# The first step of a recurrence before a feed-forward block: idle products out, two levels in one PSUM tile, three loads moved

## The chip, the cores and the metric

The kernel runs on one core of a Trainium2 chip. The metric is the device time of one execution in microseconds (us). Engines are named as in the profile: PE is TensorE (PEld its weight loads), DVE is VectorE, ACT is ScalarE, POOL is GpSimd, SP is SyncE, which here only issues DMAs.

## The reference, cut to what matters

A recurrence with decay for 4 batches, 8 heads, 768 tokens and head dimension 48, followed by a gated feed-forward block on its output.

```python
for t in range(S):
    cur = einsum('bhd,bhe->bhde', u * k[t], v[t])
    y[t] = einsum('bhd,bhde->bhe', r[t], state + cur)
    state = w[t][..., None] * state + einsum('bhd,bhe->bhde', k[t], v[t])
x = y laid out as (B * S, H * D) = (3072, 384)
h = x @ w_in                      # 384 -> 2048
g = h * erf(softplus(h))
out = g @ w_out                   # 2048 -> 384
```

## The kernel before, in words

The work is cut into 12 steps. A step holds 128 tokens (`C`) of two batches, 16 head matrices in all, in eight pairs of heads (`JP`), two heads side by side on the partitions. R, K and the decay w of a step lie with the head dimension on the partitions and the tokens along the free axis. The pairs are split into two halves, one for each batch (`j` 0 and 1).

The products of tokens with earlier tokens of the same chunk of 64 are made in six levels (`LOG = 6`). At level n the tokens fall into blocks of 2^n; the right half of a block is multiplied with its left half. For this `level_products` (matmuls at L552) writes 64 x 32 products for each pair, head and chunk to a PSUM tile `pp`; `scale` (L321 for step 0, L328 later) then multiplies R of the right halves and K of the left halves in place by running products of w, so that the next level's products carry the right decay. `take_level` brings the level's products into the SBUF tile `own`: up to level five with a masked DVE copy (L562), at level six with two ACT copies (L569). Level one uses other operands, `rk1`, in which R or K are multiplied by u, and is taken with a DVE multiplication by a mask (L774). The running products of w (`tot_sb`) are made on POOL by `totals` (L350), each behind a one-element copy `wait_for` (L769) which waits for a scale on DVE.

PSUM tiles come from `products`, which hands out two tiles in turn (`pp0`, `pp1`).

Step 0 has a function of its own, `attend_first`. It goes through the levels, then turns K by eight PE transposes (L816) into PSUM, copies the result to `kT` (half on ACT, half on DVE, L821), multiplies `own` with v into `y` (`from_own`, L584), makes the state products K x v (L659), applies the state of the first chunk to the second (`through_state`, L610) and leaves the last part of that (`hop`, three matmuls at L625) and the state of the second chunk to step 1. `fence` copies a few elements of `y` to `seen` (L593) and so waits until `from_own` is done.

Between these operations step 0 holds matmuls whose result nobody reads. `stay_warm` (L862) multiplies an identity; it stands six times at the start and twice after each half of level one. `keep_busy` (L871) multiplies zeros into the next PSUM tile; it stands after each of the levels two to five and before the transposes.

The weights w_in and w_out come as 64-bit floats and are converted on the chip: `convert` has stages that load a pair of blocks ("l"), scale its high words on ACT ("b"), its low words on ACT ("r"), shift on DVE ("h") and add on POOL ("o"). A load can be put behind an element of some tile: a one-element copy on POOL or ACT (L240, L238) into the buffer makes the DMA wait for it. A pair is 0.79 MB in two DMAs; three pairs fit into the buffers.

From step 1 on, `attend` runs the same levels, and pieces of `hidden` (w_in products, L1027) of the step before stand between them. Every engine's order of work is the order of the program text; nothing is reordered. All loads named here are issued by SP from one queue, in order.

Of the kernel before, what the change touches and what calls it, by code (L numbers as in the profile page):

```python
# [17 lines left out]
P = 128  # L18
# [43 lines left out]
def kernel(  # L62
# [68 lines left out]
    def products(shape, n=None):  # L131


        if n is not None:
            return ps_p.tile(shape, FP32, name=f"pp{n}")
        n = turns["next"]
        turns["next"] = 1 - n
        return ps_p.tile(shape, FP32, name=f"pp{n}")
# [10 lines left out]
    def load_w(s):  # L149
        ws[s] = ins.tile([P, JP, C], FP32, name="w")  # L150
        nc.sync.dma_start(out=ws[s][:], in_=rkw[s][:, 2])
# [34 lines left out]
    def load_v(s):  # L186

        vt = loaded[s][1]
        nc.sync.dma_start(out=vt[:], in_=v[s])
# [122 lines left out]
    def scale(s, level, batch=None):  # L312
# [16 lines left out]
            halves, halves, view(tots[level - 1], 0, [[1, n], [2, nb], [0, half]])  # L329
        )  # L330

    def plan_totals(s):


        tots, pairs, tot = [], [], ws[s][:].rearrange("p n t -> p (n t)")
        tot_sb = att.tile([P, JP * (C - NC)], FP32, name="tot_sb")
        used = 0
        for level in range(1, LOG + 1):
            tots.append(tot)
            nb = JP * C >> level  # L340
            new = tot_sb[:, used : used + nb]
            pairs.append((new, tot.rearrange("p (n two) -> p n two", two=2)))
            tot = new
            used += nb
        ready[s] = *ready[s], tots, tot

        def go_on(*levels, part=slice(None)):
            for level in levels:
                new, pair = pairs[level - 1]
                nc.gpsimd.tensor_mul(new[:, part], pair[:, part, 0], pair[:, part, 1])  # L350

        return go_on
# [183 lines left out]
    def first_pair(x, n):  # L536

        return turns["first"][:, n // NP, x, n % NP]
# [19 lines left out]
    def take_level(own, pp, level):  # L558
        half = 1 << (level - 1)
        got = pp[:].rearrange("p e n t -> p (e n) t")  # L560
        if level <= MASKED:
            nc.vector.copy_predicated(  # L562
                rights(own[:], half),
                rights(mask_sb[:, level - 1 : level, :].to_broadcast([P, NH, HC]), half),
                got[..., : HC // 2].rearrange("p n (b h) -> p n b h", h=half),
            )
        else:
            for s0 in range(0, C, HC):
                nc.scalar.copy(own[s0 : s0 + half, :, half:], got[s0 : s0 + half, :, :half])  # L569
# [28 lines left out]
    def through_state(s, xT):  # L598

        c, in_t, _, _, S, _, _ = parts_of(s)  # L600
        for h, state in enumerate((S, middle)):
            if not (c or h):
                continue
            t = slice(h * HC, (h + 1) * HC)
            for j, q in ((0, 2), (1, 2), (1, 0), (0, 0)) if not s else np.ndindex(NJ, NP // 2):
                q = q if not s else 2 * q
                for e in range(NE):
                    for p in (q + e, q + 1 - e):
                        n = j * NP + p
                        nc.tensor.matmul(  # L610
                            y[at(e, p), e, p // 2, j, t],
                            lhsT=state[rows(e), n, :],
                            rhs=(in_t[:, 0, n] if s else first_pair(0, n))[rows(e), t],
                            start=False, stop=True, skip_group_check=True,
                        )

        y3 = att.tile([P, UNIT], FP32, name="y3", bufs=1)
        nc.scalar.copy(y3[:].rearrange("p (j t) -> p j t", j=NJ), y[:, 1, 1])
        parts = y[:, 0, 0], y[:, 0, 1], y[:, 1, 0]
        by_kk = [xT[:, kk, :].rearrange("p (j t) -> p j t", j=NJ) for kk in range(KT)]  # L620
        if not s:

            def hop():
                for kk in range(KT):
                    nc.tensor.matmul(  # L625
                        parts[kk], lhsT=apart[:, kk],
                        rhs=y3[:].rearrange("p (j t) -> p j t", j=NJ),
                        start=False, stop=True, skip_group_check=True,
                    )
                for kk in range(KT):  # L630
                    nc.scalar.copy(by_kk[kk], parts[kk])
                stages["l"](3, xT[:, KT - 1, 0:1], True)
                stages["l"](4)
                load_w(2)

            turns["hop"] = hop
            return
        for kk in range(KT):
            nc.scalar.copy(by_kk[kk], parts[kk])
        by_scalar = {(kk, 1) for kk in range(KT) if s <= DIRECT}  # L640
        for kk in range(KT):
            n = D // KT
            for e in range(NE):
                queue = nc.scalar if (kk, e) in by_scalar else nc.sync
                queue.dma_start(
                    out=xT[e * EP + D : (e + 1) * EP, kk, :],
                    in_=y3[e * EP + kk * n : e * EP + (kk + 1) * n, :],
                )
# [97 lines left out]
    def attend_first(xT):  # L746
# [10 lines left out]
        pp = products([P, NE, JP, HC])  # L757
        for half in halves:
            level_products(pp, by_pair(made), 1, half)
            stay_warm(2)  # L760
        nc.scalar.copy(first[:], mask_sb[:, 0, :])
        totals(1, part=slice(0, batch))
        for j in range(NJ):
# [3 lines left out]
        def wait_for(t):  # L767

            nc.gpsimd.tensor_copy(out=block_sb[:, 0:1], in_=t5[:, 1, 0, NP - 1, t : t + 1])  # L769
# [9 lines left out]
        for level in range(2, LOG):  # L779
            pp = turns.pop("pp", None) or products([P, NE, JP, HC])  # L780
            for j, half in enumerate(halves):
                level_products(pp, first_pair, level, half)
                scale(0, level, batch=j)
            turns["pp"] = products([P, NE, JP, HC])
            keep_busy(turns["pp"], (DM,))
            take_level(own, pp, level)
            wait_for(1 << level - 1)
            if level == 2:
                totals(2, part=slice(batch // 2, batch))
            else:  # L790
                totals(*behind[level])
            if level == 2:
                stages["b"](0, 0)
                stages["b"](0, 1)
                stages["r"](0)
                for _ in prepare(1):
                    pass
                nc.sync.dma_start(out=vt[:], in_=v[0])
                stages["l"](1, own[:, 0, 2:3])
                nc.sync.dma_start(out=ws[1][:], in_=rkw[1][:, 2])  # L800
        totals = plan_totals(1)
        pp = turns.pop("pp")
        for j, half in enumerate(halves):
            level_products(pp, first_pair, LOG, half)
            scale(0, LOG, batch=j)
        take_level(own, pp, LOG)

        kT = att.tile([P, NH, D], FP32, name="kT", bufs=1)
        kT_by_e = kT[:].rearrange("p (e n) d -> p e n d", e=NE)
        turned = [products([P, NE, JP, HC])]  # L810
        keep_busy(turned[0], (DM,))
        for j, half in enumerate(halves):
            if j:
                turned.append(products([P, NE, JP, HC]))
            for i, n in enumerate(half):
                nc.tensor.transpose(  # L816
                    turned[j][:, 0, 2 * i : 2 * i + 2], first_pair(1, n), ident[:]
                )
        from_own(0, own, 1)
        for half, ps, copy in zip(halves, turned, (nc.scalar.copy, nc.vector.tensor_copy)):  # L820
            copy(  # L821
                kT_by_e[:, :, half.start : half.stop],
                ps[:, 0].rearrange("p (n e) d -> p e n d", e=NE)[..., :D],
            )
        stages["b"](1, 0)
        stages["b"](1, 1)
        fence()
        stages["l"](2, seen[:, 0:1])
        load_v(1)
        stages["h"](0)  # L830
        stages["h"](0)
        ps = [[products([P, NE, JP, HC], 1 - e)[:, e] for e in range(NE)]]
# [4 lines left out]
        stages["r"](1)  # L837
        stages["h"](1)
        stages["h"](1)
        wait_for(HC - 1)  # L840
        stages["o"](0)
        nc.gpsimd.tensor_mul(faded[1][:], middle[:], ends[:, :, 1:2].to_broadcast([P, JP, D]))
        totals(1)
# [14 lines left out]
    def stay_warm(times):  # L858

        for _ in range(times):  # L860
            ps = ps_m.tile([P, NC, P], FP32, name="m")
            nc.tensor.matmul(  # L862
                ps[:], lhsT=ident[:], rhs=ident[:, None, :].to_broadcast([P, NC, P]),
                start=True, stop=True,
            )

    def keep_busy(pp, columns=(DM, DM // 2)):

        zeros = states[1][0][:].rearrange("p n d -> p (n d)")
        for n in columns:  # L870
            nc.tensor.matmul(  # L871
                pp[:].rearrange("p e n t -> p (e n t)")[:, :n], lhsT=ident[:],
                rhs=zeros[:, :n], start=True, stop=True, skip_group_check=True,
            )
# [722 lines left out]
```

## Time and profile before

| | us |
|---|---|
| median of 3 runs | 585.62 |
| lowest, highest | 584.13, 586.57 |
| the profiled execution | 586.88 |
| its span | 585.1 |

| busy in the span | share |
|---|---|
| PE | 99% |
| DVE | 78% |
| ACT | 61% |
| POOL | 47% |

The profiled execution is one run; its own time is 1.8 us longer than the span from the first to the last instruction. The lines of its page give busy times. A line of the timeline gives the start and the length of a group of like instructions in us from the start of the span, then engine, line, operation, output and inputs, shape and count; where the engine stood idle before it, a bracket gives for how long and what ended the wait ("issue": nothing that the profile shows). A matmul of fp32 counts as two passes in the counts of the trace, a transpose as one.

### The profile page before, as it was taken

What the parts mean: (1) busy time and instruction counts of PE and PEld (TensorE: products, weight loads), DVE (VectorE), ACT (ScalarE), POOL (GpSimd) and SP (SyncE); (2) the same over time, 40 slices, a digit from 0 to 9 for tenths busy, and PEclk for the clock granted to TensorE, in tenths of its full rate; (3) what the DMA queues carried; (4) which work ended last, traced back from release to release, by engine and by line L of the source; (5) the groups of instructions that cost most, each with busy time, mean ns of one, the idle gap of its engine ahead of it and who ended that gap; (6) DMA issues with size and microseconds to landing.
All of it is one profiled execution on the core that took longest, in us unless ns stands there. A gap on an engine that the chain in (4) does not pass through costs nothing.

```text
span 585.1 us, 16663 instructions
## 1 busy us (share of the span) xinstructions
PE 576.4 (99%) x7240; PEld 495.1 (85%) x7240; DVE 454.7 (78%) x558; ACT 355.6 (61%) x478; POOL 274.1 (47%) x313
## 2 busy tenths in 40 slices
PE   8899999999999999999999999999999999999997
PEld 6588887688668758998898898898898899988997
DVE  6776886999996899799799799799799637256630
ACT  3658877644544598756766666665765771387700
POOL 4557391702398469659459459449549200000000
PEclk9999999999999999999999999999999999999999
DMA  8587571440433414334334334334331301000000
GB/s 269 177 273 281 201 235 44 183 154 10 145 95 116 117 55 156 63 116 165 74 111 169 74 108 172 75 108 136 74 108 55 74 8 36 2 0 2 28 27 29
DMA packets 54082, 63.25 MB, mean 108 GB/s; under 512 B 35160, under 2 KB 40568, under 8 KB 52984
## 3 DMA queue, kind: packets, MB, share of 16 engines
q1 hardware_dynamic: 53624, 61.98, 33.4%
q8 instruction: 57, 0.93, 0.6%
q10 hardware_dynamic: 384, 0.20, 0.1%
q14 instruction: 17, 0.14, 0.1%
HBM read 52.39 MB, written 8.69 MB: 104 GB/s over the span
## 4 chain that ended last, share of the span: by engine, by line
PE 95%; DVE 3%; issue 1%; ACT 0%; POOL 0%; DVEq 0%; POOLq 0%
PE m L1027 36%; PE m L1142 28%; PE m L1059 8%; PE pp L552 6%; PE pp L1230 4%; PE y L1230 2%; PE y L584 2%; PE pp L659 2%; PE y L610 2%; PE m L862 1%; PE pp L871 1%; PE pp L938 1%; DVE in L328 1%; DVE words L467 1%; PE pp L1142 0%
## 5 line engine op out<-in xcount | busy, mean ns | idle before, releaser
L1027 PE MATMUL m<-xT,w_in_sb 128*128 128x256 f32 x960 | 215.3, 382 | 0.1
L1027 PEld LDWEIGHTS m<-xT,w_in_sb 128*128 128x128 f32 x960 | 179.9, 190 | 26.2 <-issue 1.0
L328 DVE TENSOR_TENSOR in<-in,tot_sb 128x1024 f32<-128x1024 f32 (+1 forms) x55 | 75.3, 1369 | 16.5 <-PE pp L552 13.2
L463 POOL TENSOR_TENSOR rk<-words 128x528 f32<-128x528 f32 (+3 forms) x28 | 42.5, 1517 | 91.2 <-DVE sums L453 80.7
L1036 ACT COPY h<-m 128x512 f32<-128x512 f32 x80 | 46.4, 579 | 57.6 <-PE m L1027 57.5
L467 POOL TENSOR_TENSOR words<-words,rest 128x528 f32<-128x528 f32 (+10 forms) x77 | 78.1, 1015 | 6.0
L1059 PE MATMUL m<-w_out_sb,h 128*128 128x384 f32 x192 | 64.3, 491 | 0.0
L1059 PEld LDWEIGHTS m<-w_out_sb,h 128*128 128x128 f32 x192 | 35.7, 190 | 23.5
L1142 PE MATMUL m<-mixed,h 128*128 128x192 f32 x256 | 45.6, 331 | 0.0
L1142 PE MATMUL m<-w_out_sb,h 128*128 128x192 f32 x256 | 44.8, 329 | 0.0
L552 PEld LDWEIGHTS pp<-in 48*64 48x64 f32 (+1 forms) x2368 | 33.4, 126 | 12.0 <-issue 6.2
L1142 PEld LDWEIGHTS m<-mixed,h 128*128 128x128 f32 x256 | 41.4, 190 | 0.9
L1142 PEld LDWEIGHTS m<-w_out_sb,h 128*128 128x128 f32 x256 | 41.6, 190 | 0.3
L1142 PE MATMUL m<-w_out_sb,room 128*128 128x192 f32 x240 | 41.5, 326 | 0.0
L983 ACT ACT_TABLE_LOAD x30 | 38.5, 1283 | 2.7 <-issue 2.2
L987 ACT ACT_TABLE_LOAD x30 | 38.5, 1283 | 1.5 <-DVE room L1125 1.1
L1142 PEld LDWEIGHTS m<-w_out_sb,room 128*128 128x128 f32 x240 | 39.4, 190 | 0.0
L402 POOL TENSOR_TENSOR tot_sb<-tot_sb 128x256 f32<-128x256 f32 (+4 forms) x50 | 36.2, 724 | 3.8
L552 PE MATMUL pp<-in 48*64 48x32 f32 (+1 forms) x2368 | 37.3, 212 | 0.6 <-DVE in L328 0.5
L463 POOL TENSOR_TENSOR words<-words 128x336 f32<-128x336 f32 (+6 forms) x49 | 35.3, 720 | 3.8
L453 DVE TENSOR_REDUCE sums<-rk 128x14 f32<-128x672 f32 (+9 forms) x54 | 34.7, 701 | 0.0
L453 DVE TENSOR_REDUCE sums<-words 128x6 f32<-128x288 f32 (+8 forms) x66 | 26.9, 464 | 3.9 <-POOL words L463 3.6
(198 smaller groups left out, 951.5 us busy)
## 6 DMA issues: line engine op xcount, KB each, us to landing
in<-in_rkw SPq DMA_DIRECT2D x8, 1024.0 KB, 5.1
words<-in_moe_w_in SPq DMA_DIRECT2D x16, 384.0 KB, 5.4
words<-in_moe_w_out SPq DMA_DIRECT2D x16, 384.0 KB, 4.7
words<-in_rk_rows SPq DMA_DIRECT2D x8, 768.0 KB, 5.6
w<-in_rkw SPq DMA_DIRECT2D x11, 512.0 KB
v<-in_v SPq DMA_DIRECT2D x12, 384.0 KB, 5.6
out<-o SPq DMA_DIRECT2D x23, 192.0 KB, 2.4
in<-in_rkw SPq DMA_DIRECT2D x7, 512.0 KB, 5.7
```

The costliest lines, as they stand in the source:

```text
L328: nc.vector.tensor_mul(halves, halves, view(tots[level - 1], 0, [[1, n], [2, nb], [0, half]]))
L402: nc.gpsimd.tensor_mul(new, pair[:, :, 0], pair[:, :, 1])
L453: nc.vector.tensor_reduce(out=view(sums[:], n, [[near * (NEAR + 1), NEAR // near], [NEAR + 1, near - n]]), in_=terms[n], axis=mybir.AxisLi ...
L463: engine.tensor_mul(terms[n], r[:, :, n:], k[:, :, : near - n])
L467: engine.tensor_mul(k[:, :, :m], k[:, :, :m], w[:, :, n : n + m])
L552: nc.tensor.matmul(to, lhsT=rk(1, n)[rows(e), s0 : s0 + m], rhs=right, start=True, stop=True,)
L983: nc.scalar.activation(sp_room, chunks[0], AF.Softplus)
L987: nc.scalar.activation(at, sp_room, AF.Erf)
L1027: nc.tensor.matmul(ps[:, ff, :], lhsT=w_in_sb[:, g * FG + f + ff, kk * P : (kk + 1) * P], rhs=xT[:, kk, :], start=kk == 0, stop=kk == KT - 1,)
L1036: nc.scalar.copy(h[:, f : f + FT, :], ps[:])
L1059: nc.tensor.matmul(ps[j][:], lhsT=gs[g][:, f, j * C : (j + 1) * C], rhs=w_out_sb[:, g * FG + f, :], start=g + f == 0, stop=g == NG - 1 and ...
L1142: nc.tensor.matmul(to, lhsT=a[:, f], rhs=b[:, f], start=start and f == 0, stop=f == FG - 1, skip_group_check=True,)
```

## The change

- The two `stay_warm` products after each half of level one are removed, as are the `keep_busy` products before level six and before the transposes.
- Level six writes its products to the unused half of level five's PSUM tile (`pp[:, :, :, 32:]`) instead of a tile of its own.
- The last scale is split: K first, for each half (`scale_last(K=True)`), and R later, only for the second chunk's right half, which is all that is read afterwards.
- Level six is brought into `own` before level five, level five's copy stands behind K's scales, and R's scale behind that copy.
- All eight transposes go to one PSUM tile, a bank for each half.
- The load of w of step 1 is issued before the second pair of w_in blocks instead of after it. The third pair of blocks waits for the first element of `kT` instead of `seen`. v of step 1 is loaded in `hop`, after w of step 2, instead of after the third pair.
- The `wait_for` before the first weight addition looks at token 127 instead of 63.

```diff
+    def scale_last(K, batch=0):
+        half, nb = 1 << (LOG - 1), 2 * NP
+        of, tot = turns["first"][:, batch], ready[0][1][LOG - 1]
+        if K:
+            keys = view(of, NP * C, [[2 * half, nb], [1, half]])
+            nc.vector.tensor_mul(
+                keys, keys, view(tot, 2 * batch * nb + 1, [[2, nb], [0, half]])
+            )
+            return
+        queries = view(of, 3 * half, [[2 * NP * C, NJ], [C, NP], [1, half]])
+        nc.vector.tensor_mul(
+            queries, queries, view(tot, 2, [[2 * nb, NJ], [4, NP], [0, half]])
+        )
...
                 stages["l"](3, xT[:, KT - 1, 0:1], True)
                 stages["l"](4)
                 load_w(2)
+                load_v(1)
...
             level_products(pp, by_pair(made), 1, half)
-            stay_warm(2)
...
-            turns["pp"] = products([P, NE, JP, HC])
-            keep_busy(turns["pp"], (DM,))
-            take_level(own, pp, level)
+            if level < LOG - 1:
+                turns["pp"] = products([P, NE, JP, HC])
+                keep_busy(turns["pp"], (DM,))
+                take_level(own, pp, level)
...
                 nc.sync.dma_start(out=vt[:], in_=v[0])
+                nc.sync.dma_start(out=ws[1][:], in_=rkw[1][:, 2])
                 stages["l"](1, own[:, 0, 2:3])
-                nc.sync.dma_start(out=ws[1][:], in_=rkw[1][:, 2])
         totals = plan_totals(1)
-        pp = turns.pop("pp")
+        last = pp[:, :, :, HC // 2 :]
         for j, half in enumerate(halves):
-            level_products(pp, first_pair, LOG, half)
-            scale(0, LOG, batch=j)
-        take_level(own, pp, LOG)
+            level_products(last, first_pair, LOG, half)
+            scale_last(K=True, batch=j)
+        take_level(own, last, LOG)
+        take_level(own, pp, LOG - 1)
+        scale_last(K=False)
...
-        turned = [products([P, NE, JP, HC])]
-        keep_busy(turned[0], (DM,))
+        turned = products([P, NE, JP, HC])
         for j, half in enumerate(halves):
-            if j:
-                turned.append(products([P, NE, JP, HC]))
             for i, n in enumerate(half):
                 nc.tensor.transpose(
-                    turned[j][:, 0, 2 * i : 2 * i + 2], first_pair(1, n), ident[:]
+                    turned[:, j, 2 * i : 2 * i + 2], first_pair(1, n), ident[:]
                 )
         from_own(0, own, 1)
...
+        stages["l"](2, kT[:, 0, 0:1])
         stages["b"](1, 0)
         stages["b"](1, 1)
         fence()
-        stages["l"](2, seen[:, 0:1])
-        load_v(1)
...
-        wait_for(HC - 1)
+        wait_for(C - 1)
```

## The prediction

> **What bounds the kernel now.** I read the page's busy shares first, then the busy times of three stretches, then the timelines of PE and DVE in the first 30 us.
>
> ```profile
> PE 576.4 (99%) x7240; PEld 495.1 (85%) x7240; DVE 454.7 (78%) x558; ACT 355.6 (61%) x478; POOL 274.1 (47%) x313
> ...
> 7.10:20.60 13.50, 12.82 (x405) 9.14 (x405) 12.11 (x17) 6.95 (x17) 5.43 (x14) 1.00 0.82 261
> 20.60:29.90 9.30, 6.68 (x208) 5.30 (x205) 4.58 (x10) 5.53 (x13) 6.76 (x6) 1.00 0.44 150
> 29.90:60.90 31.00, 30.99 (x664) 25.71 (x666) 21.00 (x22) 21.66 (x35) 19.24 (x25) 1.00 0.75 261
> ```
>
> The stretches list PE, PEld, DVE, ACT, POOL, the granted clock, the DMA share and GB/s. From 29.9 us PE is full (30.99 of 31.00), and over the whole span it is 99% busy. So what step 0 saves before the first piece of `hidden` (L1027 at 29.89) arrives at the end one for one, unless step 1 can't feed PE. Inside step 0 PE's fullness is false: part of it is idle products (L862, L871), and DVE is busy 12.11 of 13.50.
>
> ```profile
> 9.76 1.23 DVE L774 TENSOR_TENSOR own<-pp,first 128x1024 f32<-128x1024 f32 x1 [0.77 <-PE pp L552]
> 11.41 1.30 DVE L321 TENSOR_TENSOR in<-in,tot_sb 128x512 f32<-128x512 f32 x2 [0.42 <-PE pp L552]
> ...
> 17.61 1.34 DVE L321 TENSOR_TENSOR in<-in,tot_sb 128x512 f32<-128x512 f32 x2
> 18.87 0.70 DVE L562 COPY_PREDICATED own<-mask_sb,pp 128x512 f32<-128x512 int32 x1
> 19.48 1.27 DVE L321 TENSOR_TENSOR in<-in,tot_sb 128x512 f32<-128x512 f32 x2
> 21.57 0.56 DVE L821 COPY kT<-pp 128x384 f32<-128x384 f32 x1 [0.82 <-PE pp L816]
> ```
>
> Two waits for PE stand before level two; after them DVE runs without a gap to 20.75, 1.93 us a level (13.77, 15.71, 17.61, 19.48). Now PE after the levels:
>
> ```profile
> 18.73 0.76 PE L552 MATMUL pp<-in 48*32 48x32 f32 x64
> 19.72 0.88 PE L871 MATMUL pp<-s,ident 128*128 128x384 f32 x2 [0.24 <-DVE own L562]
> 20.44 1.09 PE L816 MATMUL pp<-ident,in 128*128 128x128 f32 x8
> 21.46 0.66 PE L584 MATMUL y<-own,v 64*48 64x64 f32 x32
> 22.27 0.65 PE L659 MATMUL pp<-v,kT 64*48 64x48 f32 x20
> 23.81 0.43 PE L659 MATMUL pp<-v,kT 64*48 64x48 f32 x11 [0.88 <-issue]
> ...
> 29.40 0.56 PE L552 MATMUL pp<-rk 48*64 48x64 f32 x18 [1.26 <-issue]
> ```
>
> PE stops twice in the middle of a group, for nothing that the profile names. Between the two stops the timeline counts 128 matmuls (12 and 32 to through 24.7, 32 of L610, 32 of L552, 6 of L625, 14 of L552), each with its weight load: 256 instructions.
>
> **What the Trainium skill says.** "Runtime: NRT & Kernel Launch", Instruction fetch mechanics: instructions come in blocks of 16 KiB (256 of them), fetched while the block before is executed, at a cost "mostly hidden". The trace agrees on the block and not on the hiding: the page's queue q8 moves 57 packets of 0.93 MB, and narrow windows of the DMA view find one of them starting at 15.7, 21.6, 27.0 and 32.5; PE resumes 2.2 and 2.4 us after the second and third. "DMA: Bandwidth & Descriptors", Queues, rings and completion order: a DMA engine takes turns between queues, a packet at a time. The trace fits: with loads in flight the third and fourth packets come 3.2 and 3.1 us after PE entered the block before (23.81, 29.40). "SBUF — State Buffer", Who interferes with whom: a DVE operation with two SBUF inputs and a POOL read exclude each other. Here the first scale of level one took 1.12 us beside POOL, its twin 0.68. "TensorE: Matmul & The Clock Gate", Part 1: PE falls to half clock after about an idle window of 3.4 us. The clock here is 1.00 throughout, and no stretch that the change opens is over 1 us but by a stall.
>
> **The change, part by part** (clock of the profiled execution).
>
> *Idle products at level one.* Four matmuls of two passes, 1.06 us a pair in the chain, 2.12 us of PE. Level one then ends at 8.6 instead of 9.6; level two needs DVE's scale of level one, which ends at 9.00 as before (it waits for w, landed 7.2). `own` (L774) starts at 9.0, not 9.76, and the level-two scale follows it: its first half by 10.1 instead of 11.41. DVE's chain moves **1.3 us** earlier, not 2.1. POOL's totals of level two are ready at 10.2 and later ones hang on DVE, so they move along.
>
> *Levels five and six in one tile.* The idle product between them goes (0.84), and its wait for the level-four copy. Level five's scale is done at 17.6; level six runs 17.0 to 18.2 (19.5 before). K's two scales are 128x256 each, 0.42 by the row of that shape (L372) against 0.67, and end at 18.7; the transposes end at 19.4 (21.5 before). But the order of writes to `own` turns round: level six's ACT copies (2 x 0.58) come first, and DVE's level-five copy, which overlaps them, must wait. ACT is free at 18.3, as before, since it multiplies step 1's R and K from 14.6 on, when they land. So: ACT copies to 19.4, level-five copy 19.5 to 20.2, R's scale (256 elements, 0.42) to 20.5, kT's DVE copy to 21.0; `from_own` 20.3 to 20.95, `seen` 21.05. The state products start at 21.1 instead of 22.27: still **1.15** early. Level six's own gain is eaten by its ACT copies; behind the waiting DVE copy stand R's scale, the kT copy and `seen`.
>
> *Transposes in one tile*, and R scaled only in the second half: one bank wait less, 0 us; the idle product before them (0.84) was cover.
>
> *Three loads.* w of step 1 is issued at 10.6 instead of 17.13, ahead of the second weight block; that block at about 13.9; the third behind the first kT copy, at about 20 instead of 22.64, through POOL's 0.18 us copy, which waits there with nothing due behind it. v of step 1 goes from 23.50 to behind `load_w(2)`. None is waited for on the path: w is used at 25.7, v at 52.6. They shift DMA traffic against the instruction blocks. After the change 10 to 12 passes fewer stand before the block boundaries, so these fall at level six's fifth matmul, at the end of the state products, and in step 1's level one.
>
> *If every block came in time*: state products to 22.2; ACT `b(1)` to 22.7, middle to 23.2; rest of `through_state` to 23.8; ACT's r(1) and y3 to 24.5; the three hop products to 26.1; xT to 27.05; first piece at 27.1 instead of 29.89, **2.8 us**.
>
> *But the boundary in level six.* Its block is requested when the sequencer enters level four, at about 13.2 to 13.8, and w now flows until about 16 (1.96 MB from 10.5 at the 0.36 MB/us of that stretch). By the traced delays it starts between 1.2 us (lightly loaded: 14.5 to 15.7) and 3.2 us later and is usable 2.2 us after that: 16.6 to 19.2, against 17.05 needed. I cost it at a stall of 1.3 (bounds 0 and 2.5). The following blocks find a quieter DMA queue (the second weight block ends by 18.5) and are then just in time: the 0.88 and most of the 1.26 stay saved. 2.8 less 1.3, less 0.2 for what remains, is **1.3 us**.
>
> *Step 1.* DVE and PE run there without slack: level five's products (45.32) follow the scale that ends 45.26, which follows a shift waiting for ACT and a weight load landed 42.3. v adds 0.39 MB (1.1 us) behind the hop; DMA has idle room at 36 to 38. Cost 0 to 0.7; taken as within the rounding.
>
> Sum: 586.88 less 1.3 is 585.6 for the profiled execution, which stands 1.26 above the median of 585.62; from the median, **584.3 us**.
>
> **The rivals.**
> (B) No stall at level six, none later: 2.8 us, **582.8**. For it: the sequencer may run ahead of the waits (the 15.7 packet served 17.89 just in time). Against: w in flight where before the queue had emptied at 14.9.
> (C) The other side: the stall at level six lasts 2.5 us, since level six is on the path of K's scales, transposes and state products. These then start at 23.4, 1.2 later than before, and if step 1's block stalls too (the old 1.26), the first piece starts at 30.4: +0.5, **586.1**. It decides from a block usable later than about 19, with the next stall uncovered.
> (D) The gain is real and step 1's weight stream gives it back: v and w2 delay the block for level five by about 1 us, leaving 0.3: **585.3**.
> That the idle products kept the clock up is no case of its own, since no idle window is long enough; it stands behind the chance of slower.
>
> **How the numbers follow.** 0.5% of this kernel, 2.9 us, is about what a measurement can tell from no change. Chances: likeliest 0.52 (own range 583.2 to 585.4), B 0.27, C 0.13, D 0.08. Runs shown spread from 584.1 to 586.6, so each case is blurred by about 0.8. The range takes B with that blur below and C above: 582.2 to 586.5. Faster by over 0.5% (below 582.7) is half of B and a little of A: 0.16; slower, beyond 588.5, only C together with a lost clock: 0.04; within, 0.80.
>
> **What would show it.** Right: the level-two scale near 10.1; level five's copy behind ACT's; state products by 21 to 22.5; no `issue` gap inside L659's group; the first piece 28 to 29. Wrong: PE's gap of `issue` in level six absent (B) or over 2 us (C), a clock below 1.00 before 30 us, or an equal shift at 30 us that is gone at 60 (D).

## The result, and the profile after

The change makes the kernel **slower**: 590.42 us (median of 7 runs, 587.61 to 591.81) against 584.53 (7 runs, 584.12 to 586.57), a ratio of 1.0085, interval 1.0066 to 1.0103. The forecast was 584.3, in the range 582.2 to 586.5: wrong in size and in sign. The profiled execution of after, 587.61, is the quickest of its seven, so its trace shows less than the median's loss; a second one, below, shows more. The ratios and counts of clocks below leave out three runs of two kernels (592.51, 593.01 and 593.41 us), each over 1.5% above the fastest of its kernel, and since their mean clocks (0.979 and 0.980) are as low as those of after, the losses of these two may be a little larger than stated.

The page of after has lost 1% of PE's share. The busy times of after in the same three stretches that were shown for before (same columns: PE, PEld, DVE, ACT, POOL, clock, DMA share, GB/s) say that the clock is no longer whole in the first two. First the page's line, then the stretches:

```profile
PE 573.6 (98%) x7228; PEld 493.7 (84%) x7228; DVE 457.1 (78%) x559; ACT 355.0 (61%) x478; POOL 272.2 (46%) x313
```

```profile
7.10:20.60 13.50, 9.88 (x373) 7.36 (x363) 11.80 (x21) 6.84 (x17) 5.22 (x15) 0.94 0.79 278
20.60:29.90 9.30, 8.40 (x211) 6.86 (x210) 5.58 (x10) 5.42 (x13) 6.23 (x6) 0.91 0.28 88
29.90:60.90 31.00, 28.82 (x617) 23.84 (x618) 20.41 (x21) 20.81 (x33) 19.29 (x25) 1.00 0.76 274
```

PE works 9.88 of 13.50 us where it had been busy 12.82, and 28.82 of 31.00 in step 1 where it had been full. The clock of 0.94 and 0.91 comes from one window of half clock, which the clock record places at 18.94, for 3.41 us. DVE's timeline of after:

```profile
9.47 1.21 DVE L790 TENSOR_TENSOR own<-pp,first 128x1024 f32<-128x1024 f32 x1
10.60 1.28 DVE L321 TENSOR_TENSOR in<-in,tot_sb 128x512 f32<-128x512 f32 x2
...
16.78 1.34 DVE L321 TENSOR_TENSOR in<-in,tot_sb 128x512 f32<-128x512 f32 x2
19.34 0.79 DVE L339 TENSOR_TENSOR in<-in,tot_sb 128x256 f32<-128x256 f32 x2 [1.22 <-PE pp L568]
20.90 0.71 DVE L578 COPY_PREDICATED own<-mask_sb,pp 128x512 f32<-128x512 int32 x1 [0.77 <-ACT own L585]
...
22.33 0.56 DVE L837 COPY kT<-pp 128x384 f32<-128x384 f32 x1 [0.40 <-ACT kT L837]
```

DVE's waits for PE ahead of level two are gone, and its level-five scale (17.61 before) starts at 16.78. Then DVE waits 1.22 us for level six and 0.77 for ACT's copies. PE shows why (timeline of after; L568 is the level products, L832 the transposes, L600 `from_own`, L676 the state products, L1042 the pieces of `hidden`):

```profile
17.53 0.31 PE L568 MATMUL pp<-in 48*32 48x32 f32 x10 [0.40 <-DVE in L321]
18.78 0.88 PE L568 MATMUL pp<-in 48*32 48x32 f32 x54 [0.94 <-issue]
19.82 1.97 PE L832 MATMUL pp<-ident,in 128*128 128x128 f32 x8 [0.16 <-DVE in L339]
21.71 0.95 PE L600 MATMUL y<-own,v 64*48 64x64 f32 x32
22.94 0.88 PE L676 MATMUL pp<-v,kT 64*48 64x48 f32 x30 [0.28 <-DVE kT L837]
...
28.48 2.86 PE L1042 MATMUL m<-xT,w_in_sb 128*128 128x256 f32 x12
...
40.65 1.13 PE L568 MATMUL pp<-in 48*64 48x32 f32 x64 [0.76 <-DVE in L328]
...
45.93 1.14 PE L568 MATMUL pp<-in 48*64 48x32 f32 x64 [1.36 <-DVE in L328]
```

Level six stops for 0.94 us after 10 of its 64 passes. The transposes run at half clock: 1.97 us instead of 1.09. The first piece still starts at 28.48 (29.89 before), 1.4 us early against this first profile of before. Step 1 takes that back: PE stops 0.76 and 1.36 us for the scales ahead of levels four and five, and level five stands at 45.93 (45.32 before).

### The profile page after: what moved, and what is told of

It is laid out like the page before. It is cut to its first block, busy times and chain, and to the rows that moved or that the text cites. A ratio compares the mean times of both kernels' runs of the same rounds, so it can differ in the third digit from the quotient of the medians.

```text
span 585.8 us, 16636 instructions
## 1 busy us (share of the span) xinstructions
PE 573.6 (98%) x7228; PEld 493.7 (84%) x7228; DVE 457.1 (78%) x559; ACT 355.0 (61%) x478; POOL 272.2 (46%) x313
## 4 chain that ended last, share of the span: by engine, by line
PE 71%; DVE 9%; issue 1%; DMA 1%; POOL 1%; ACTq 0%; ACT 0%; POOLq 0%; DVEq 0%
PE m L1157 28%; PE m L1042 25%; PE m L1074 5%; PE pp L1245 4%; PE y L1245 2%; PE pp L568 2%; DVE in L328 2%; PE y L600 2%; PE y L626 1%; PE pp L676 1%; DVE words L483 1%; DVE rk L479 1%; DVE sums L469 1%; DMA rest<-in_w_rows 1%; DVE h L1031 1%
## 5 line engine op out<-in xcount | busy, mean ns | idle before, releaser
L1042 PE MATMUL m<-xT,w_in_sb 128*128 128x256 f32 x960 | 215.2, 382 | 0.3
L1042 PEld LDWEIGHTS m<-xT,w_in_sb 128*128 128x128 f32 x960 | 179.8, 190 | 26.4 <-ACT h L1051 0.9
L328 DVE TENSOR_TENSOR in<-in,tot_sb 128x1024 f32<-128x1024 f32 (+1 forms) x55 | 76.8, 1397 | 15.6 <-PE pp L568 14.0
L568 PEld LDWEIGHTS pp<-in 48*64 48x64 f32 (+1 forms) x2368 | 33.8, 126 | 15.5 <-DVE in L328 4.9
L568 PE MATMUL pp<-in 48*64 48x32 f32 (+1 forms) x2368 | 37.6, 212 | 4.4 <-DVE in L328 2.3
```

The costliest lines, as they stand in the source:

```text
L328: nc.vector.tensor_mul(halves, halves, view(tots[level - 1], 0, [[1, n], [2, nb], [0, half]]))
L568: nc.tensor.matmul(to, lhsT=rk(1, n)[rows(e), s0 : s0 + m], rhs=right, start=True, stop=True,)
L1042: nc.tensor.matmul(ps[:, ff, :], lhsT=w_in_sb[:, g * FG + f + ff, kk * P : (kk + 1) * P], rhs=xT[:, kk, :], start=kk == 0, stop=kk == KT - 1,)
```

## The experiments

The theory after this reading had two parts: the **clock**, which the idle products held up, and the **weight stream** of step 1, which the moved loads delay. The rivals: that the new order of levels and scales costs the time, and that late blocks of instructions (stops of PE for `issue`, read as in the prediction) do. Where a mean clock is given below, one half window of 3.41 us takes about 0.003 of it; "whole" is 0.999 or more. Ratios are to before, measured beside each kernel.

**The two halves of the change, from both sides.** Four kernels: the changed one with its idle products back; the changed one with its loads back; before with only the idle products out; before with only the three loads moved.

```diff
+            stay_warm(2)                     # idle back: after each half of level one,
+        keep_busy(turned, (DM,))             # ahead of level six and of the transposes
```

```diff
-                stages["l"](1, own[:, 0, 2:3])   # loads moved: w ahead of the second pair,
                 nc.sync.dma_start(out=ws[1][:], in_=rkw[1][:, 2])
+                stages["l"](1, own[:, 0, 2:3])
...
+        stages["l"](2, kT[:, 0, 0:1])            # the third pair behind kT,
         stages["b"](1, 0)
         stages["b"](1, 1)
         fence()
-        stages["l"](2, seen[:, 0:1])
-        load_v(1)
...
                 load_w(2)
+                load_v(1)                        # and v behind w of step 2
```

> The changed kernel with its idle products put back (two pairs of stay_warm after level one, keep_busy before level six and before the transposes, both into the tile that the transposes use later); levels, scales, transposes and loads stay as changed. Clock theory (the idle products had kept PE's clock up, and the loss is windows of half clock): mean clock 0.999 in every run as in the kernel before, no half-clock window in step 0, and the time falls from 590 to 585 or less. Load theory (the loss is step 1's weight blocks, which now land late): little change, 587 to 590, with the stops before levels four and five of step 1 still there. Order theory (the order of the copies into own costs it): also no change.

> The changed kernel with the three loads where they were before; no idle products. Load theory: the stops before levels four and five of step 1 (0.76 and 1.36 us) go, the gain of 1.4 us at step 1's first piece is kept or shrinks by PE's instruction stalls, time 584 to 587. Clock theory: still half-clock windows, mean clock 0.98 to 0.997 and 588 to 592.

> The kernel before with nothing changed but the idle products taken out (stay_warm twice after level one, keep_busy before level six and before the transposes). Clock theory: this alone brings the half-clock windows, mean clock 0.98 to 0.997, and most of the loss: 587 to 591. Load theory: as before or faster by up to 1.3 us, 583 to 585.

> The kernel before with nothing changed but the three loads moved. Load theory: DVE's shifts of step 1 wait for their weight blocks and the time rises by 1 to 3 us, to 586 to 588, at a clock of 0.999. Clock theory: no loss, 584 to 585; by the fetch part of the prediction the two issue stalls of 0.88 and 1.26 us shrink, so at best 583.

| | median us (runs) | ratio, interval | whole clock |
|---|---|---|---|
| after, idle products back | 586.71 (5) | 1.0036 [1.0024, 1.0048] | 5 of 5 |
| after, loads back | 587.75 (22) | 1.0044 [1.0025, 1.0064] | 6 of 20 |
| before, idle products out | 588.71 (7) | 1.0058 [1.0028, 1.0089] | 0 of 6 |
| before, loads moved | 586.39 (10) | 1.0031 [1.0016, 1.0045] | 9 of 10 |
| after | 590.42 (7) | 1.0085 [1.0066, 1.0103] | 0 of 7 |

Idle products out alone cost 0.58%, loads moved alone 0.31%; their sum, 0.89%, agrees with the 0.85% of the whole. The clock goes with the idle products, taken out of before or put back into after. With the loads moved and the clock whole, the loss sits where after had it, ahead of level five of step 1 (timeline of before with the loads moved):

```profile
45.06 1.13 PE L552 MATMUL pp<-in 48*64 48x32 f32 x64 [1.06 <-DVE in L328]
```

That scale on DVE follows a shift, the shift waits for ACT, and ACT waits for a block of weights. ACT's timeline, first of this execution and then of the second profile of before (below), shows that it gets the block 1.27 us later:

```profile
42.02 0.86 ACT L255 ACTIVATE y<-words 128x768 f32<-128x768 f32 x1 [2.81 <-DMA words<-in_moe_w_in]
40.75 0.87 ACT L255 ACTIVATE y<-words 128x768 f32<-128x768 f32 x1 [1.73 <-DMA words<-in_moe_w_in]
```

The 0.31% is measured over ten runs; its place is read from one execution. Such stops do not come from the moved loads alone: with the loads as before, PE stopped 1.06 us ahead of level four in after with its loads back, and 1.40 us in before with the small idle products (below).

**Before once more, and the parts of the loads.** The kernel before unedited; w of step 1 alone moved; v alone moved; the changed levels, scales and transposes with idle products and loads as before; and the third pair alone moved, with v still directly behind it. The single moves are the three pieces of the second diff. The kernel with the changed structure is after with its idle products put back (the first diff) and its loads back.

> The kernel before, unchanged, for a second profile: the first one took 586.88 us, while the median of 32 of its runs is 584.83. If the two issue stalls of step 0 (0.88 and 1.26 us) are there in every execution, they show again and step 1's first piece starts near 29.9 us; if they belong to the slow tail, at least one is gone and the first piece starts at 27.5 to 29.

> The kernel before with one load moved: w of step 1 ahead of the second pair of weight blocks. Fetch theory (w in flight holds up the instruction block that level six needs): a stop of PE of 0.5 to 1.5 us at level six, and 0.3 to 1.5 us slower in all. If the cost of the moved loads lies in step 1's weight stream: no change within 0.2%, since this load is not part of that stream.

> The kernel before with one load moved: v of step 1 behind w of step 2 in the hop. Weight-stream theory: its 0.39 MB stand among the weight blocks of step 1, the block for level five lands about 1 us late, PE stops before level four or five for about 1 us, and the time rises by 0.5 to 1.5 us. Fetch theory: no loss, perhaps 0.5 us gained, since PE's instruction block behind the state products waits no longer behind v.

> The changed levels, scales, order of copies and transposes with the idle products put back and the three loads where they were: what the rest of the change is worth alone. By the prediction's step: level six up to 0.7 us earlier, but the copies into own in the other order give that back, so 0 to 0.5 us faster at a clock of 1.00 (584.3 to 584.8 against 584.8). If the turned order of the copies costs: 0.3 to 1 us slower.

> The kernel before with the third pair of weight loads issued behind the first kT copy instead of behind seen, and v of step 1 directly after it. The moves of w alone and of v alone came out at +0.03% and +0.06%, all three together at +0.31%. If the third pair's place is the cost: +0.2 to +0.3% (585.4 to 586.0 beside 584.2), with a stop of 0.5 to 1.1 us on DVE's scale L328 ahead of levels four or five of step 1. If it is only the sum of traffic (no one load alone): within 0.1%, and the loss of the three is that of their combination. Rival, the load earlier in the queue helps: -0.1% or less and no stop. The clock stays 1.00 in all three.

The second profile of before came to 584.56. In its PE timeline neither stop of the first profile is there:

```profile
22.38 1.02 PE L659 MATMUL pp<-v,kT 64*48 64x48 f32 x31
...
28.24 2.86 PE L1027 MATMUL m<-xT,w_in_sb 128*128 128x256 f32 x12
...
43.80 1.14 PE L552 MATMUL pp<-in 48*64 48x32 f32 x64
```

The first piece starts at 28.24 and level five of step 1 at 43.80, 1.65 and 1.52 us ahead of the profile that the forecast was made from. **The two stops of 0.88 and 1.26 us are in one execution of this kernel and not in the other.** Such stops come and go: before with the third pair moved stopped for 1.65 us at the same place (29.22). Measured against the second profile, after gained nothing even at the first piece (28.48).

The single loads: w 584.37 us, 1.0003 [0.9992, 1.0014]; v 584.6, 1.0006 [0.9995, 1.0017]; the third pair 585.16, 1.001 [0.9996, 1.0024]. None alone can be told from nothing; their sum, 0.19%, lies within the interval of the three together. Which load costs what stays open. The changed structure, 584.81, 1.0005 [0.999, 1.002], costs and brings nothing that can be measured: that rival is out.

**Which idle products hold the clock.** Before, with only those at level one out; only the later two out; and with one product instead of two after each half.

```diff
-            stay_warm(2)                     # the first kernel; in the third,
+            stay_warm(1)                     # this in its place
...
-            keep_busy(turns["pp"], (DM,))    # the second kernel, stay_warm(2) kept
+            if level < LOG - 1:
+                keep_busy(turns["pp"], (DM,))
...
-        keep_busy(turned[0], (DM,))
```

> The kernel before with only the idle products at level one (2.12 us of PE) left out. Clock theory, level one decides: the clock falls to half at 9 to 13 us in some or most executions, means of 0.98 to 0.997, and the median is 0.3 to 0.6% slower (586 to 587.7); busy PE in 7.1 to 20.6 falls from 12.8 to about 10.7. Rival, the clock hangs on the products at the end of the levels alone: clock 1.00 in all runs, the state products about 1.3 us early, and the median -0.1 to -0.2% (583.0 to 583.6), less what later stops take back. Rival, idle products never mattered and the spread has another source: clock as often below 1.00 as in before (never).

> The kernel before with only the two later idle products left out (ahead of level six and ahead of the transposes, 1.7 us of PE), the ones at level one in place. Clock theory, these two decide: the clock falls to half for one or more windows of 3.4 us from about 18 to 19 us, mean 0.980 to 0.997, and the median is 0.2 to 0.6% slower. Rival, level one decides: the clock is 1.00 in all runs and the median within 0.1% of before, since DVE sets the pace of these levels. If only both together lower the clock, both this and the kernel without the level-one products keep 1.00.

> The kernel before with half of the idle products at level one: one matmul after each half instead of two (1.06 us of PE out, 1.06 left). Without any of them 12 of 22 runs fell below clock 0.998, with all of them 5 of 59. Clock theory with a bound on how much PE works in a window of 3.4 us: a share between, some 15 to 45% of the runs, and a median 0 to 0.3% above before. If any idle product at the place is enough: a share as in before and, the chain of DVE being 0.5 to 0.9 us earlier, a median 0 to 0.15% below before, which would be the one version ahead of both kernels. If the share is as without any (half or more): the bound lies above this amount, 0.4% or more slower.

Level one out: 588.7 us, 1.0053 [1.0031, 1.0076], 10 of 22 runs whole, median 584.9 in those and 588.65 to 591.63 in the others. The later two out: 585.43, 1.0015 [1.0003, 1.0028], 6 of 22 whole, most others with a single window (585.1 to 586.4). Half at level one: 585.15, 1.0006 [0.9996, 1.0015], **22 of 22 whole**. So both places matter, and half of the products is enough at the first. It is still no faster, as the runs at whole clock without any were not (584.9 beside 584.26). In the execution with half of them, the transposes start at 19.85 (20.54 in the second profile of before), and a block of instructions then comes late (its timeline):

```profile
27.95 0.45 PE L552 MATMUL pp<-rk 48*64 48x64 f32 x14 [0.56 <-issue]
```

**What a typical execution of after looks like.** After again, twice; before without the level-one products again; after with the loads back again; one execution each.

> The changed kernel, unedited, for a second profiled execution: the first (587.61) was the quickest of seven and shows one half-clock window of 3.41 us, which cannot be the 5.9 us of the median. If the clock carries the rest, an execution of 589 to 592 has four to seven such windows in one run from about 9 to 13 us on, ends step 0 about 3 to 5 us later than the first profile, and shows no other loss beyond the two stops of about 1 us in step 1. If the rest is a later loss, the clock shows one or two windows and the difference grows after 46 us.

> The same again, a third profiled execution, since which windows are granted at half speed differs between executions: same expectations as for the second; together they say whether the fall begins at the level-one products (9 to 13 us) or at the transposes (about 19 us).

> The kernel before without the idle products at level one, unedited, for a second profiled execution. Ten of its 22 runs had a mean clock of 0.986 to 0.988, four or five windows, which the first profile (one window, at 30.28, after a stop of 1.76 us) does not show. If the level-one products are what is missing, the windows begin at 9 to 13 us. If a late block of instructions is the trigger in these too, they begin behind a stop of over 1 us at 26 to 29 us. An execution at full clock would come to 584.5 to 585.4 and show where the 0.9 us gained at the transposes is lost.

> The changed kernel with the loads as before, unedited, for a second profiled execution. By the clock theory its time follows the number of half-clock windows: 584 to 586 with none, 587 to 588 with one or two, 590 to 591 with six or seven. Rival: the time is set by the weight blocks of step 1 alone, and goes with the stops ahead of levels four and five, whatever the clock.

After came to 591.26 and 586.22, the third kernel to 589.96, the fourth to 588.3, beside 583.94 for before. The execution of 591.26 is near the median of after. Its clock falls at 10.59 and stays at half for six windows, to 31.07 (busy times in that stretch, and PE's timeline):

```profile
10.60:31.10 20.50, 20.22 (x435) 15.47 (x435) 13.64 (x23) 9.48 (x20) 7.59 (x16) 0.50 0.48 172
```

```profile
8.53 1.27 PE L568 MATMUL pp<-in 48*64 48x32 f32 x64 [0.27 <-DVE in L321]
10.36 1.40 PE L886 MATMUL pp<-s,ident 128*128 128x384 f32 x2 [0.56 <-POOL tot_sb L366]
11.69 1.93 PE L568 MATMUL pp<-in 48*64 48x32 f32 x64
13.56 1.65 PE L886 MATMUL pp<-s,ident 128*128 128x384 f32 x2
...
21.91 1.97 PE L832 MATMUL pp<-ident,in 128*128 128x128 f32 x8
```

Ahead of the fall PE has no wait over 0.56 us. After it a level takes 1.93 us instead of 1.14, an idle product 1.65 instead of 0.91; PE is now busy 20.22 of 20.50 and sets the pace in DVE's place. Against the second profile of before, this execution is 1.4 us behind at the transposes (21.91 and 20.54), 4.0 at the first piece of `hidden` (32.25 and 28.24), 5.5 at level five of step 1 (49.30 and 43.80) behind two stops (0.57 and 1.15), and 6.7 at the end. The last 1.2 need not come from the change: behind level five the first profile of before loses 0.9 to the second as well. The execution of 586.22 has one window, at 19.28, behind a 1.22 us stop in level six; it is 0.3 behind at the first piece and 1.6 at the end.

The third kernel has four windows, from 11.92 to 25.57, so here too the fall begins behind level one.

The fourth kernel has its window elsewhere: behind a late block (1.72 us, its PE timeline) the clock is at half from 29.70, although `hidden` keeps PE full there.

```profile
28.61 0.34 PE L568 MATMUL pp<-rk 48*64 48x64 f32 x5 [1.72 <-issue]
```

So late blocks, the last rival, may have a share in some executions, but the long falls need none: no `issue` stop of PE stands ahead of those at 10.59 and 11.92, nor ahead of the window at 18.64 in the first profile of after with its loads back. Nor is such a stop enough: 1.26 us in the first profile of before and 1.65 with the third pair moved were followed by no half window.

**Busy time or the size of the array; and a version ahead of both?** Before with its level-one products on a 48x48 corner of the identity; and the changed structure with the loads as before, half of the level-one products and the one ahead of level six.

```diff
-            stay_warm(2)
+            stay_warm(2, 48)     # lhsT=ident[:48, :48], rhs=ident[:48, None, :], into ps[:48]
```

```diff
+            stay_warm(1)                     # the changed kernel, loads as before
...
+        turned = products([P, NE, JP, HC])
+        keep_busy(turned, (DM,))             # ahead of level six
```

> The kernel before with its idle products at level one kept in number, place and length, but with a 48x48 corner of the identity as the fixed operand instead of 128x128, so that PE is as busy and 14% of the array's cells work. If the granted clock goes by how long PE is busy: as before, clock 1.00 in over 9 of 10 runs and a median within 0.15%. If it goes by how much of the array works (the count of rows times columns times streamed elements per window of 3.41 us, which fell from about 0.40 to 0.30 of full idle products at that place when they were left out): clock below 0.998 in a third to two thirds of the runs, as without them (12 of 22), with windows of half clock from 8 to 12 us on, and a median 0.3 to 0.6% slower.

> The changed levels, scales and transposes with the loads as before, half of the idle products at level one (one after each half) and the one ahead of level six kept, the one ahead of the transposes out. By the array's work per window (0.25 to 0.32 in the changed kernel at levels one and six, about 0.36 to 0.44 here): clock 1.00 in nearly all runs, and 583.6 to 584.8, 0 to 0.15% ahead of before, if step 1 keeps what step 0 gains; level with before if late blocks of instructions or weights take it back, as they did with half the products in the kernel before. Rival, the shorter step 0 itself lowers the clock: below 0.998 in a third of the runs and 0.2% or more slower.

The small products: 584.38 us, 0.999 [0.9978, 1.0002], 21 of 22 runs whole. A small array holds the clock as well; its size does not decide at this place. PE's busy time goes with the counts there, as far as one execution of each can say. The stretch from 7.10 to 12.00 holds 4.90 us of it in before; without the level-one products (first execution), and with the small ones, it holds

```profile
7.10:12.00 4.90, 3.45 (x145) 2.50 (x137) 4.90 (x11) 0.99 (x4) 2.22 (x5) 1.00 0.77 226
```

```profile
7.10:12.00 4.90, 4.42 (x142) 3.19 (x136) 4.90 (x11) 1.09 (x4) 2.23 (x6) 1.00 0.80 235
```

3.45 goes with 12 of 22 runs below whole, 4.42 with one of 22, and the half-sized group (4.50) with none; before itself, at 4.90, had 5 of 59. But busy time is not the whole rule: among the windows of 3.41 us at full clock, those followed by half clock were busy for 0.29 to 0.80 of their length, and others with 0.54 and 0.63 were not followed by it. **What exactly is counted stays open.**

The second kernel did not come out as expected: 587.43, 1.0033 [1.0016, 1.0049], 3 of 16 whole. Part of this is the edit's own: taking the idle product back allocated a second tile, so that the transposes fell into the tile of levels five and six and waited for its last reader (its PE timeline):

```profile
19.09 0.72 PE L568 MATMUL pp<-in 48*32 48x32 f32 x60 [0.86 <-issue]
21.91 1.94 PE L834 MATMUL pp<-ident,in 128*128 128x128 f32 x8 [2.10 <-DVE own L578]
```

So it doesn't answer what it was made for. No version ran ahead of before by more than its interval.

## Why the prediction was wrong

- **The clock.** The step that failed reads "that the idle products kept the clock up is no case of its own, since no idle window is long enough". It was the largest term. After and the same kernel with its idle products back differ by 1.0085 against 1.0036, about 2.9 us; before loses 0.58%, 3.4 us, by the idle products alone. "TensorE: Matmul & The Clock Gate", Part 1, was used for an idle window of 3.4 us. The length of the window agrees (the half stretches are 3.41, 10.24, 13.65 and 20.48 us, one, three, four and six of it), but no idle window was needed. The same page, "A second HAM failure mode: psum-queue depth-cycling", says that short idle times between groups of matmuls can also make the clock swing; the execution of 591.26 is of that kind, with waits of 0.27 and 0.56 us ahead of the fall. The prediction did not hold that section against the trace: it called PE's fullness in step 0 false, which was right, and costed the work that made it so only as time.
- **The sum's base.** The likeliest case had the "0.88 and most of the 1.26" saved, and put the execution's 1.26 us above the median aside as a constant. The second profile has neither stop and is 1.52 us ahead at level five of step 1, so most of that saving was of something that another execution does not lose. The median was a weak base too: 585.62 came from three runs, seven gave 584.53 and the later comparisons of several runs 584.18 to 584.83, so that a forecast of 584.3 was hardly a gain. Nor did a lead at the first piece arrive "one for one": with the changed structure alone it starts at 27.87, 0.37 ahead of the second profile of before, and the span is 583.0 beside 582.7. What takes it back is not resolved by these single executions.
- **Step 1's weight stream.** This was case D, "v and w2 delay the block for level five by about 1 us", at 0.08; the likeliest case called it 0 to 0.7, "within the rounding". It measured 0.31%, 1.8 us; in the five traces with the three loads moved PE stops 0.32 to 1.36 us ahead of level five. The place was right and the size too small: with a first piece that is no earlier, there was no gain for it to eat. That v and w of step 2 are what delays the block is not shown, since v alone measured 1.0006.
- **Right**: level two's scale, forecast at 10.1, starts at 10.14 in the execution of 591.26, and at 10.60 in the first profile of after, where DVE had waited longer for its first loads and level one's scale started 0.55 later than in the first profile of before (7.83 and 7.28); ACT's copies come before DVE's level-five copy; level six stops behind its fifth matmul in two of three traces of after, 0.94 and 1.22 us where 1.3 was costed; there is no `issue` gap in the state products; the first piece at 28.48 and 28.50 in these two, inside "28 to 29" (32.25 in the execution of 591.26). State products start at 22.94, not by 22.5; the transposes ahead of them took 1.97 us at half clock instead of 1.09. As "Runtime: NRT & Kernel Launch", Instruction fetch mechanics, was read with its block of 256 instructions, the stop was placed to the matmul. (The "1.93 us a level" is 1.90 by the starts that it gives.) Getting the structure right was worth nothing: that part by itself measured 1.0005.
- **The chances.** Slower was held to need case C "together with a lost clock", 0.04. A clock that the profile shows as 1.00 throughout says that it was held, not by what; a change that removes the only work with no other purpose had to carry the clock as a case, with a price from records already at hand (the idle products at the start of before, ahead of its clock record, stand 0.43 us apart, later ones 0.22).

## What to carry to other kernels

Idle matmuls in a stretch of short waits may be holding TensorE's clock. Before removing them, count PE's busy time per few microseconds without them, and price the stretch at half speed. Take a second profile of the kernel before, and strike every stop that is not in both, since a gain built on one execution's stops may not be there in the next. A load moved out of the way of one stage has to be followed to the stage that waits for its neighbours.

## What had not been expected of the hardware

- In the execution of 591.26 the clock falls to half with no wait of PE over 0.56 us ahead of it. Falls last one to six windows of 3.41 us in the traces compared here; before too has runs below a whole clock, 5 of 59 in one comparison.
- At half clock the levels fill PE (20.22 of 20.50 us busy), and the clock still does not come back for six windows. In other traces it came back after a single half window (after: PE busy 3.26 of 3.42 us in it). Nor does it wait for the pieces of `hidden`: it was whole again at 31.07 and 25.57, ahead of first pieces at 32.25 and 32.22. What brings it back is open.
- A late block of instructions of 1.72 us was followed by a half window in a stretch that is full of work; one of 1.65 us was not.
- Which execution gets which windows and stops differs from run to run: the same changed kernel took from 586.22 to 591.81 us.
